# 32x32 block transposes on VectorE with a reorder through DRAM, in place of TensorE transposes, in an attention and feed-forward kernel; and one pinned order behind step 30

## The chip, the cores and the metric

The kernel runs on one core of a Trainium2 chip. TensorE (PE in the profile; PEld is its weight loads) writes its products to PSUM; VectorE (DVE), ScalarE (ACT) and GpSimd (POOL) work on tiles, each in the order of its own instruction stream; SyncE (SP) issues the transfers between DRAM and SBUF, also in order. The metric is the device time of one execution in microseconds, 657.18 us before the change.

## The reference

Attention in chunks, then a feed-forward layer with a rational activation, all in float32:

```python
for c in range(nc):                       # chunks of 32 queries
    q_c = q[:, :, c_start:c_end]
    k_full = concat([mem_k, k[:, :, l_start:r_end]])   # 8 + up to 16 + 32 + 8 keys
    scores = scale * (q_c @ k_full.T)
    a = exp(scores - max(scores)); a = a / (sum(a) + 1e-09)
    out[:, :, c_start:c_end] = a @ v_full
x = out.transpose(0, 2, 1, 3).reshape(3072, 512)
h = x @ w_in                              # 512 x 2048
P = a[0] + a[1]*h + a[2]*h**2 + a[3]*h**3
Q = 1 + abs(b[0])*abs(h) + abs(b[1])*h**2
y = (P / (Q + 1e-6)) @ w_out              # 2048 x 512
```

There are 4 batches of 8 heads, 768 positions and head size 64.

## The kernel before

**Blocks, units, steps.** The 3072 rows are cut into eight blocks of 384. A block needs its attention output, transposed, as four tiles of 128 channels by 384 rows; each comes from one unit, which is a pair of heads (i, p): block i, pair p. A step n is one pair of a block and a slice j of 128 of the 2048 hidden features; `order` lists the 128 steps: ten slices of block 0, ten of block 1, all 16 of block 2, the rest of blocks 1 and 0, and then blocks 3 to 7, 16 steps each (block 3 begins at step 48, block 7 at step 112).

**One step.** `g1(n)` is a set of 12 matmuls (`h`, L368): four channel tiles by three products, since x and w are each split into a high and a low part of type float32r, and low by low is left out. A chain then makes the activation out of h, 128x384, in these parts: `chain_abs` (ACT: ha = |h|, L419, and cy from it, L420), `chain_below` (POOL: cy times ha, L424), `chain_line` (ACT: ct, L429), `chain_above` (DVE, L433, L434), `chain_inverse` (ACT: Ln, L438, then Exp, L439), `chain_ratio` (DVE: L443 to L445), `chain_hi` (POOL: ghi, L450) and `chain_lo` (POOL: glo = ct - ghi, L457). `g2(n)` is a set of nine matmuls (`o`, L383), three for each 128 rows: ghi by w_hi, ghi by w_lo, glo by w_hi. They add up over a block's slices in three banks of PSUM; at a block's end `evac` takes them to the output.

**One unit.** `b` (`att_scores`, L264): 12 matmuls, one for each chunk of 32 queries, each on a strip of 32 columns of TensorE (`tile_position=(0, j * CHUNK)`), into one bank as 128x384; chunk c goes to strip c mod 4 (`g, j = divmod(c, 4)`). `m` (`att_max`): DVE masks, takes the maximum, subtracts. `x` (`att_exp`): ACT. `c` and `k` (`att_turn`, L291, and `att_keep`, L296): three 128x128 transposes on TensorE into PSUM and a copy by ACT give eT. `d` (`att_values`, L306): 12 matmuls on strips, as in b. `n` (`att_norm`): three DVE instructions give xt. `e` (`att_back`, L324): three TensorE transposes into PSUM. `h` (`att_hi`, L328): ACT rounds to x_hi. `l` (`att_lo`, L339): DVE takes x_lo = x - x_hi. Units of block 3 and later read q and k from one SBUF slot, and v from two buffers, loaded by SP.

**What sets the order.** Up to step 29 a list written out by hand (`SEQ`) gives the order of every instruction, and `pin` holds it. It covers the attention of blocks 0 to 2. From `HAND = 30` on each step emits `g1(n + 1)`, the chain's parts for n, n - 1 and n - 2, the units' stages that `plan` has put there (from `BASES`, `EARLY`, `OFFS` and, for block 5 on, `first[i] - LEAD + 4 * p`, four steps apart) and `g2(n - 2)`; there the instructions have priorities only, and the scheduler of the tile framework decides the order on each engine and in SP's queue.

Of the kernel before, what the change touches and what calls it, by code (L numbers as in the profile page):

```python
# [12 lines left out]
F32 = mybir.dt.float32  # L13
# [3 lines left out]
ALU = mybir.AluOpType  # L17
# [34 lines left out]
GHI_POOL = 200  # L52
LOAD_AT = [-2, -1]
EARLY = {1: [0, 1, 2, 3], 2: [0, 2, 2, 2], 3: [0, 1, 1, 3], 4: [0, 2, 3, 6]}
# [5 lines left out]
OFFS = [0, 3, 4, 4]  # L60
BASES = {1: [-2, 0, 1, 2], 2: [4, 6, 8, 10], 3: [34, 36, 40, 42], 4: [38, 45, 49, 54]}
# [3 lines left out]
def attn_moe(ctx, tc, qk, vm, w, a, b, out):  # L65
# [125 lines left out]
    def x_move(store):  # L191
        for d, t in zip(x_keep, (xh[0], xl[0])):
            if store:
                load(d.bitcast(F32), t.bitcast(F32))
            else:
                nc.gpsimd.dma_start(out=t, in_=d)
# [50 lines left out]
    turn = [0]  # L247

    def pa(i):
        turn[0] = (turn[0] + 1) % 4  # L250
        if i == 0:
            if turn[0] == 3:
                return ps_r.tile([P, 512], F32, name="pa", tag="cr")
            return ps_o.tile([P, DM], F32, name="pa", tag=f"o{turn[0]}")
        return ps_a.tile([P, 512], F32, name="pa", tag="pa0" if pinned[0] else "pa")

    def att_scores(i, p):
        u = unit[i, p]
        users[qk_slot(i, p)] = users.get(qk_slot(i, p), 0) - 1
        s = u["s"] = pa(i)  # L260
        sv = s[:, :NG * 2 * KEYS].rearrange("x (g h w) -> x g h w", g=NG, h=2)
        for c in range(NC):
            g, j = divmod(c, 4)
            pin(nc.tensor.matmul(sv[j * CHUNK:(j + 1) * CHUNK, g], lhsT=u["q"][c],  # L264
                                 rhs=u["k"][c], start=True, stop=True, tile_position=(0, j * CHUNK)))
# [19 lines left out]

    def att_turn(i, p):
        u = unit[i, p]
        ep = u["ep"] = pa(i)
        e = u.pop("e")
        for g in range(NG):  # L290
            pin(nc.tensor.transpose(out=ep[:, g * P:(g + 1) * P], in_=e[:, g], identity=ident))  # L291

    def att_keep(i, p):
        u = unit[i, p]
        eT = u["eT"] = at.tile([P, TB], F32, name="eT", tag="eT")
        pin(nc.scalar.copy(eT, u.pop("ep")[:, :TB]))  # L296

    def att_values(i, p):
        u = unit[i, p]
        if i == 0 and p >= 2:  # L300
            users[V_SLOTS[p - 2]] -= 1
        o = u["o"] = pa(i)
        ov = o[:, :NG * 2 * (D + 1)].rearrange("x (g h d) -> x g h d", g=NG, h=2)
        for c in range(NC):
            g, j = divmod(c, 4)
            pin(nc.tensor.matmul(ov[j * CHUNK:(j + 1) * CHUNK, g],  # L306
                                 lhsT=u["eT"][:, c * CHUNK:(c + 1) * CHUNK], rhs=u["v"][c],
                                 start=True, stop=True, tile_position=(0, j * CHUNK)))
# [10 lines left out]
    def att_back(i, p):  # L319
        u = unit[i, p]  # L320
        xp = u["xp"] = pa(i)
        xt = u.pop("xt")
        for g in range(NG):
            pin(nc.tensor.transpose(out=xp[:, g * P:(g + 1) * P], in_=xt[:, 2 * g:2 * g + 2, :], identity=ident))  # L324

    def att_hi(i, p):
        u = unit[i, p]
        pin(nc.scalar.copy(xh[i][:, p, :], u["xp"][:, :TB]))  # L328
        if i < XL_POOL:
            xf = u["xf"] = at.tile([P, TB], F32, name="xf", tag="xf")  # L330
            pin(nc.scalar.copy(xf, u.pop("xp")[:, :TB]))

    def att_lo(i, p):
        u = unit.pop((i, p))
        hi = xh[i][:, p, :].bitcast(F32)
        if i < XL_POOL:
            pin(nc.gpsimd.tensor_tensor(xl[i][:, p, :], u["xf"], hi, op=ALU.subtract))
        else:
            pin(nc.vector.tensor_tensor(xl[i][:, p, :], u["xp"][:, :TB], hi, op=ALU.subtract))  # L339

    def together(*parts):
        def f(i, p):
            for part in parts:
                part(i, p)
        return f

    att_d, att_e = together(att_values, att_norm), together(att_back, att_hi, att_lo)
    stages = [together(att_scores, att_max, att_exp), together(att_turn, att_keep), att_d, att_e]
# [22 lines left out]
    def g2(n):  # L371
# [7 lines left out]
        for t in range(NG):  # L379
            cols = slice(t * P, (t + 1) * P)  # L380
            o = outs[i][t]
            for m, (gt, wt) in enumerate(((hi, w_hi), (hi, w_lo), (lo, w_hi))):
                ins = nc.tensor.matmul(o, lhsT=gt[:, cols], rhs=wt, start=begin and m == 0, stop=end and m == 2)  # L383
                if pinned[0] or n == total - 1:
                    tc.keep_in_program_order(ins)
        if end and not pinned[0]:
            evac(i, j)

    def evac(i, j):
        for t in range(NG):  # L390
            if j < NJT - 1:
                if t == 0:
                    spare = slot(SPARES[i], "spare", F32, NG * DM)
                y = spare[:, t * DM:(t + 1) * DM]
            else:
                y = st.tile([P, DM], F32, name="stage", tag="stage")
            r = i * TB + t * P
            rows = slice(t * P, (t + 1) * P)
            if j < NJT - 1:
                pin(nc.scalar.mul(y, outs[i][t], 1.0 / W_SCALE))  # L400
                nc.sync.dma_start(out=part[i][rows, :], in_=y)
                continue
            if i < 2:
                nc.sync.dma_start(out=y, in_=part[i][rows, :])
                nc.vector.scalar_tensor_tensor(y, outs[i][t], 1.0 / W_SCALE, y, op0=ALU.mult, op1=ALU.add)
            elif i < NBLK - 1:
                nc.scalar.mul(y, outs[i][t], 1.0 / W_SCALE)
            else:
                half = DM // 2
                nc.scalar.mul(y[:, :half], outs[i][t][:, :half], 1.0 / W_SCALE)  # L410
                nc.vector.tensor_scalar(y[:, half:], outs[i][t][:, half:], 1.0 / W_SCALE, None, op0=ALU.mult)
            nc.sync.dma_start(out=out[r:r + P, :], in_=y)
        del outs[i]
# [40 lines left out]
    def chain_lo(z):  # L454
        glo = gl[z] = gp.tile([P, TB], F32R, name="glo", tag="glo")
        engine = nc.gpsimd if z < total - 1 else nc.vector
        pin(engine.tensor_tensor(glo, chain.pop(z)["t"], gh[z].bitcast(F32), op=ALU.subtract))  # L457

    def step(n):
        for lag, parts in ((2, (chain_hi, chain_lo)), (0, (chain_abs, chain_below, chain_line, chain_above)), (1, (chain_inverse, chain_ratio))):  # L460
            if 0 <= n - lag < total:
                for part in parts:
                    part(n - lag)
# [11 lines left out]
    x_free = {i: last[i - 2] - 1 if i > 1 else -2 for i in range(NBLK)}  # L475

    att, used = {}, {}

    def plan(at_step, rank, f, i, p):
        att.setdefault(at_step, []).append((rank, f, i, p))  # L480

    for i in range(3, NBLK):
        for p, base in enumerate(BASES.get(i, [first[i] - LEAD + 4 * p for p in range(NPAIR)])):
            offs = EARLY.get(i, OFFS)
            buf = qk_slot(i, p)
            at_qk = max(HAND, base + LOAD_AT[0], used.get(buf, -2))
            at_v = max(HAND, base + LOAD_AT[1], used.get(("v", p % 2), -2))
            plan(at_qk, 10, att_load, i, p)
            plan(max(at_qk, at_v), 11, att_loadv, i, p)
            floor = at_qk + 1  # L490
            for d, f in enumerate(stages):
                if f is att_d:
                    floor = max(floor, at_v + 1)
                if f is att_e:
                    floor = max(floor, x_free[i])
                floor = max(floor, base + offs[d])
                plan(floor, len(stages) - d, f, i, p)
                if d == 0:
                    used[buf] = floor
                if f is att_d:  # L500
                    used["v", p % 2] = floor
                floor += 1

    def attention_slot(n):
        for _, f, i, p in sorted(att.get(n, []), key=lambda e: (e[0], e[3])):
            f(i, p)
# [25 lines left out]
    paired = dict(b=att_scores, m=att_max, x=att_exp, c=att_turn, k=att_keep, d=att_values, n=att_norm, e=att_back, h=att_hi, l=att_lo)  # L532
    convert = dict(w=lambda key: w_load(*key), A=w_abs, B=w_bits, H=w_hi, L=w_lo)

    def hand(token):
# [3 lines left out]
        if where and kind in paired:  # L539
            paired[kind](i, p)  # L540
# [26 lines left out]
    def emit(step, offset, f, *args):  # L567
        tc.cur_priority = 8000 + 300 * step + offset
        f(*args)

    for n in range(HAND, total + LAG):
        tc.cur_priority = 8000 + 300 * n
        if n + 1 < total:
            g1(n + 1)
        step(n)
        emit(n, PA, attention_slot, n)
        tc.cur_priority = 8000 + 300 * n + 180
        if n - LAG >= 0:
            g2(n - LAG)
# [43 lines left out]
```

## Time and profile before

| | us |
|---|---|
| median of 3 executions | 657.18 (656.86 to 659.78) |
| the profiled execution, its time | 656.87 |
| its span, first to last instruction | 655.1 |
| TensorE busy (matmuls) | 628.3 (96%) |
| VectorE busy | 467.5 (71%) |
| ScalarE busy | 426.5 (65%) |
| GpSimd busy | 413.9 (63%) |
| mean granted TensorE clock | 0.987 |

The profile is of one execution. In a row of a timeline stand the start and the duration in us, the engine, the line of the kernel, the operation, out<-in, shapes, a count where instructions are merged, and in brackets the idle time ahead with what ended it. A matmul's duration is longer than its distance to the next one, since matmuls overlap: what a set costs TensorE is read from the starts. In a row of windows stand, after the length, each engine's busy time with its number of instructions, the granted clock, the share of the DMA engines that is busy and GB/s. In a row of a group stand the total busy time, the mean of one in ns, and idle time ahead. A float32 matmul of the program (not float32r) stands in the trace as two MATMUL records.

### The profile page before, as it was taken

How to read it: one execution, taken by the hardware profiler on the slowest of the kernel's cores; microseconds unless marked ns; L12 is line 12 of the kernel's file. 1: busy time of each engine (PE TensorE's matmuls, PEld its weight loads, DVE VectorE, ACT ScalarE, POOL GpSimd, SP SyncE). 2: the span in 40 equal slices, each digit the busy share in tenths (PEclk: the TensorE clock that was granted, in tenths of full speed). 3: DMA queues.
4: the chain of work that ended last, by engine and by line, in shares of the span. 5: the costliest groups of instructions: out<-in, count | busy, mean ns of one | idle time of the engine just before them, and what ended most of it. 6: DMA issues, size and time to landing. Idle time of an engine off the chain costs nothing.

```text
span 655.1 us, 12177 instructions
## 1 busy us (share of the span) xinstructions
PE 628.3 (96%) x4432; PEld 548.9 (84%) x4432; DVE 467.5 (71%) x940; ACT 426.5 (65%) x833; POOL 413.9 (63%) x439
## 2 busy tenths in 40 slices
PE   4689999999999999999999999999999999999997
PEld 3477787889988888878888888888888988999995
DVE  4878998997957577587677667666756766666664
ACT  3677878778855666466656756566656666666663
POOL 5557776878957666436665565656656565666663
PEclk8879999999999999999999999999999999999999
DMA  7998137304021524251211112213101300001001
GB/s 252 371 404 270 61 93 239 111 25 177 4 71 32 197 87 140 80 170 61 62 62 62 53 57 62 61 62 109 51 23 50 110 1 0 2 1 49 1 2 49
DMA packets 20525, 61.81 MB, mean 94 GB/s; under 512 B 3441, under 2 KB 3441, under 8 KB 20081
## 3 DMA queue, kind: packets, MB, share of 16 engines
q1 hardware_dynamic: 19856, 58.66, 26.4%
q0 software_dynamic: 288, 1.57, 0.7%
q8 instruction: 35, 0.57, 0.4%
q10 hardware_dynamic: 320, 0.80, 0.3%
q14 instruction: 26, 0.20, 0.1%
HBM read 51.58 MB, written 9.44 MB: 93 GB/s over the span
## 4 chain that ended last, share of the span: by engine, by line
PE 86%; DVE 7%; DMA 3%; issue 2%; ACT 1%; SPq 0%; DVEq 0%; ACTq 0%
PE h L368 40%; PE o L383 39%; PE pa L264 3%; PE pa L306 3%; DMA qk<-in_qk_dram 2%; PE pa L291 1%; DVE stage L169 1%; PE pa L324 1%; DVE w_raw L170 1%; DMA w_raw<-in_w_dram 1%; DVE mx L277 1%; DVE ct L433 1%; DVE ct L443 0%; DVE cr L444 0%; DVE ct L445 0%
## 5 line engine op out<-in xcount | busy, mean ns | idle before, releaser
L368 PE MATMUL h<-x_hi,w_hl 128*128 128x384 f32 x1024 | 268.5, 342 | 3.4 <-DVE ct L434 3.1
L383 PE MATMUL o<-w_hl,ghi 128*128 128x512 f32 x768 | 240.7, 398 | 0.0
L424 POOL TENSOR_TENSOR cy<-cy,ha 128x384 f32<-128x384 f32 x128 | 130.0, 1016 | 133.4 <-ACT cy L420 131.0
L368 PEld LDWEIGHTS h<-x_hi,w_hl 128*128 128x128 f32 x1024 | 187.7, 190 | 15.0 <-DVE ct L434 4.5
L368 PE MATMUL h<-x_lo,w_hl 128*128 128x384 f32 x512 | 174.1, 340 | 0.0
L383 PEld LDWEIGHTS o<-w_hl,ghi 128*128 128x128 f32 x768 | 140.2, 188 | 27.2 <-issue 4.0
L383 PE MATMUL o<-w_hl,glo 128*128 128x512 f32 x384 | 148.5, 398 | 0.0
L450 POOL TENSOR_TENSOR ghi<-ct,zero 128x384 fp32r<-128x384 f32 x127 | 105.0, 827 | 62.0 <-DVE ct L445 29.5
L457 POOL TENSOR_TENSOR glo<-ct,ghi 128x384 fp32r<-128x384 f32 x127 | 129.0, 1016 | 8.0 <-PE o L383 0.3
L443 DVE SCALAR_TENSOR_TENSOR ct<-ct,par,cr 128x384 f32<-128x384 f32 x128 | 78.2, 611 | 78.0 <-ACT cr L439 77.3
L438 ACT ACTIVATE cr<-cy 128x384 f32<-128x384 f32 x128 | 63.3, 495 | 96.2 <-POOL cy L424 65.3
L433 DVE TENSOR_TENSOR ct<-ct,h 128x384 f32<-128x384 f32 x128 | 70.2, 549 | 54.6 <-ACT ct L429 51.2
L419 ACT ACTIVATE ha<-h 128x384 f32<-128x384 f32 x128 | 62.9, 491 | 58.4 <-PE h L368 51.3
L368 PEld LDWEIGHTS h<-x_lo,w_hl 128*128 128x128 f32 x512 | 97.0, 189 | 0.4 <-issue 0.2
L420 ACT ACTIVATE cy<-ha,bab 128x384 f32<-128x384 f32 x128 | 90.6, 708 | 1.1
L429 ACT ACTIVATE ct<-h,par 128x384 f32<-128x384 f32 x128 | 85.2, 667 | 0.6 <-POOL glo L457 0.6
L383 PEld LDWEIGHTS o<-w_hl,glo 128*128 128x128 f32 x384 | 71.7, 188 | 16.4 <-issue 1.0
L434 DVE SCALAR_TENSOR_TENSOR ct<-ct,par,h 128x384 f32<-128x384 f32 x128 | 78.2, 612 | 3.0
L445 DVE SCALAR_TENSOR_TENSOR ct<-cr,ct 128x384 f32<-128x384 f32 x128 | 71.1, 555 | 3.0
L444 DVE SCALAR_TENSOR_TENSOR cr<-cy,cr 128x384 f32<-128x384 f32 x128 | 71.1, 555 | 0.4
L439 ACT ACTIVATE cr<-cr 128x384 f32<-128x384 f32 x128 | 61.2, 478 | 3.4
L183 POOL TENSOR_TENSOR w_hl<-w_raw,w_hl 128x512 fp32r<-128x512 f32 x32 | 41.9, 1311 | 23.8 <-ACT w_hl L178 22.8
(54 smaller groups left out, 422.1 us busy)
## 6 DMA issues: line engine op xcount, KB each, us to landing
qk<-in_qk_dram SPq DMA_DIRECT2D x64, 288.0 KB, 3.9
w_raw<-in_w_dram SPq DMA_DIRECT2D x26, 512.0 KB, 7.3
v_main<-in_vm_dram SPq DMA_DIRECT2D x56, 195.0 KB, 3.0
out_dram<-stage SPq DMA_DIRECT2D x24, 256.0 KB, 2.2
w_raw<-in_w_dram SPq DMA_DIRECT2D x3, 1024.0 KB, 4.8
part<-spare SPq DMA_DIRECT2D x6, 256.0 KB, 2.2
stage<-part SPq DMA_DIRECT2D x6, 256.0 KB, 2.8
v_first<-in_vm_dram SPq DMA_DIRECT2D x4, 195.0 KB, 4.4
```

The costliest lines, as they stand in the source:

```text
L368: pin(nc.tensor.matmul(h[:, :TB], lhsT=wt[:, cols], rhs=xt[i][:, ct, :], start=m == 0, stop=m == last))
L383: ins = nc.tensor.matmul(o, lhsT=gt[:, cols], rhs=wt, start=begin and m == 0, stop=end and m == 2)
L420: pin(nc.scalar.activation(c["y"], c["ha"], AF.Identity, scale=B1, bias=B0))
L424: pin(nc.gpsimd.tensor_tensor(c["y"], c["y"], c.pop("ha"), op=ALU.mult))
L429: pin(nc.scalar.activation(c["t"], c["h"], AF.Identity, scale=A3, bias=A2))
L433: pin(nc.vector.tensor_tensor(t, t, h, op=ALU.mult))
L434: pin(nc.vector.scalar_tensor_tensor(t, t, A1, h, op0=ALU.add, op1=ALU.mult))
L443: pin(nc.vector.scalar_tensor_tensor(t, t, A0, r, op0=ALU.add, op1=ALU.mult))
L444: pin(nc.vector.scalar_tensor_tensor(r, yy, QC, r, op0=ALU.add, op1=ALU.mult))
L445: pin(nc.vector.scalar_tensor_tensor(t, r, 2.0, t, op0=ALU.subtract, op1=ALU.mult, reverse0=True))
L450: pin(nc.gpsimd.tensor_tensor(ghi, chain[z]["t"], zero.broadcast_to([P, TB]), op=ALU.add))
L457: pin(engine.tensor_tensor(glo, chain.pop(z)["t"], gh[z].bitcast(F32), op=ALU.subtract))
```

## The change

For blocks 3 to 7 (`BLOCKWISE = 3`) the six TensorE transposes of a unit go. `c` and `e` each become one VectorE instruction that transposes every 32x32 block of a 128x384 tile in place of its position (`turn_blocks`), a store of the result to DRAM and four loads of 32 partitions (`across`), which put the blocks where a full transpose would have put them. So that this works out, chunk c goes to strip c // 3 in these blocks (`place`). `k` is gone; `h` reads the loaded tile; `l` moves from VectorE to GpSimd.

```diff
+BLOCKWISE = 3
+BASES = {3: [31, 33, 36, 38], 4: [42, 46, 50, 54]}
+WHEN = dict(b=0, m=0, x=1, c=1, d=5, n=5, e=6, h=9, l=9)
+SOON = {3: dict(d=4, n=4, e=5, h=8, l=8), 4: dict(h=8, l=8)}
+XB = {"xf": 2}
...
+    def place(i, c):
+        return divmod(c, 4) if i < BLOCKWISE else (c % NG, c // NG)
+
+    def across(blocks, name):
+        kept = dr.tile([P, TB], F32, name=name, tag=name, bufs=2)
+        load(kept, blocks)
+        t = at.tile([P, TB], F32, name=name, tag=name, bufs=XB.get(name, 1))
+        n = TB // 4
+        for b in range(4):
+            load(t[b * CHUNK:(b + 1) * CHUNK].rearrange("k (j n) -> k j n", n=n),
+                 kept.rearrange("(j k) (b n) -> b k j n", k=CHUNK, n=n)[b])
+        return t
...
-            g, j = divmod(c, 4)
+            g, j = place(i, c)
...
+    def turn_blocks(src):
+        t = at.tile([P, TB], F32, name="blocks", tag="blocks", bufs=2)
+        pin(nc.vector.transpose(out=t.rearrange("x (b g k) -> x b g k", b=4, g=NG), in_=src.rearrange("x g (b k) -> x b g k", b=4)))
+        return t
...
     def att_turn(i, p):
         u = unit[i, p]
+        if i >= BLOCKWISE:
+            u["eT"] = across(turn_blocks(u.pop("e").rearrange("x g w h -> x g (w h)")), "eT")
+            return
...
     def att_back(i, p):
         u = unit[i, p]
+        if i >= BLOCKWISE:
+            u["xp"] = across(turn_blocks(u.pop("xt").rearrange("x (g h) d -> x g (h d)", h=2)), "xf")
+            return
...
+        elif i >= BLOCKWISE:
+            pin(nc.gpsimd.tensor_tensor(xl[i][:, p, :], u["xp"][:, :TB], hi, op=ALU.subtract))
...
-        if z < min(GHI_POOL, total - 1):
+        if z < total - 2:
...
-        engine = nc.gpsimd if z < total - 1 else nc.vector
+        engine = nc.gpsimd if z < total - 2 else nc.vector
```

Behind step 30 everything is pinned now, the transfers too, in the order of the loop below. `attend(n, ...)` emits the stages that `WHEN` and `SOON` put at step n, counted from the unit's base; at the end of a block the loop also places `evac`, and `fetch` for the partial sums of blocks 0 and 1.

```diff
-    pinned[0] = in_order[0] = False
...
     for n in range(HAND, total + LAG):
...
+        g2(n - 2)
+        attend(n, "db")
+        attend(n, "qv")
+        if n + 1 < total - 1:
+            g1(n + 1)
...
+            chain_abs(n)
+            chain_below(n)
+            chain_line(n)
...
+            chain_above(n)
...
+            chain_inverse(n)
...
+            chain_ratio(n)
+        if n < total - 1:
+            chain_hi(n - 1)
+            chain_lo(n - 1)
+        attend(n, "xhlencm")
```

TensorE's stream in the attention of a late block, before: the three transposes of one unit (`e` is its input) between an h set and an o set, and further on the values of that unit and the scores of the next in the middle of an o set.

```order
L368 MATMUL h<-x_lo_105,w_hl 128x384
L291 MATMUL pa<-ident,e 128x128 x3
L383 MATMUL o_5289<-w_hl,ghi 128x512 x2
...
L383 MATMUL o_5290<-w_hl,ghi 128x512
L306 MATMUL pa<-v_main_101,eT 32x130 x12
L264 MATMUL pa<-qk 32x128 x12
L383 MATMUL o_5290<-w_hl,ghi 128x512
```

TensorE's stream at such a place now: the scores of one unit (L276) between an o set and an h set, and one step later the values (L328) of the unit ahead of it.

```order
L401 MATMUL o_5351<-w_hl,glo 128x512
L276 MATMUL pa<-qk 32x128 x12
L386 MATMUL h<-x_hi_103,w_hl 128x384 x2
...
L401 MATMUL o_5351<-w_hl,glo 128x512
L328 MATMUL pa<-v_main_101,eT 32x130 x12
L386 MATMUL h<-x_hi_103,w_hl 128x384 x2
```

The transposes are gone, and scores and values no longer stand next to each other; over the whole stream behind step 31, 17 such neighbours were there before and one is there now.

GpSimd's stream in the same stage, before: one of the three instructions of each step after the other, with no x_lo.

```order
L424 TENSOR_TENSOR cy<-cy,ha 128x384
L450 TENSOR_TENSOR ghi<-ct,zero 128x384
L457 TENSOR_TENSOR glo<-ct,ghi 128x384
L450 TENSOR_TENSOR ghi<-ct,zero 128x384
L424 TENSOR_TENSOR cy<-cy,ha 128x384
```

GpSimd's stream now, with x_lo of a unit (`xf` is the tile loaded from DRAM) behind the glo of every fourth step.

```order
L447 TENSOR_TENSOR cy<-cy,ha 128x384
L473 TENSOR_TENSOR ghi<-ct,zero 128x384
L480 TENSOR_TENSOR glo<-ct,ghi 128x384
L364 TENSOR_TENSOR x_lo_104<-xf,x_hi_102 128x384
L447 TENSOR_TENSOR cy<-cy,ha 128x384
L473 TENSOR_TENSOR ghi<-ct,zero 128x384
```

The order of the three is fixed: cy of step n, then ghi and glo of step n - 1; and x_lo is new there.

SyncE's queue in that stage, before: only the loads of v and of q and k, two halves each.

```order
L116 DMA v_main_100<-in_vm_dram 64x780 x2
L116 DMA qk<-in_qk_dram 64x1152 x2
L116 DMA v_main_101<-in_vm_dram 64x780 x2
L116 DMA qk<-in_qk_dram 64x1152 x2
L116 DMA v_main_100<-in_vm_dram 64x780 x2
```

SyncE's queue now; `blocks` is VectorE's output, the second eT and xf the tile in DRAM.

```order
L115 DMA qk<-in_qk_dram 64x1152 x2
L115 DMA v_main_100<-in_vm_dram 64x780 x2
L115 DMA eT<-blocks 128x384
L115 DMA eT<-eT 32x4x96 x4
L115 DMA xf<-blocks 128x384
L115 DMA xf<-xf 32x4x96 x4
```

Ten transfers a unit have come into the queue behind the loads that were there.

More of the change, by code (lines that the diff above doesn't have):

```diff
@@ L195, in x_move @@
             else:
-                nc.gpsimd.dma_start(out=t, in_=d)
+                pin(nc.gpsimd.dma_start(out=t, in_=d))
     unit = {}
@@ L383, in g2, with fetch @@
                 ins = nc.tensor.matmul(o, lhsT=gt[:, cols], rhs=wt, start=begin and m == 0, stop=end and m == 2)
[L384 to L389, printed above, removed]
-        for t in range(NG):
+                pin(ins)
+    kept = []
+    def fetch(i):
+        for t in range(NG):
+            y = st.tile([P, DM], F32, name="stage", tag="stage")
+            load(y, part[i][t * P:(t + 1) * P, :])
+            kept.append(y)
@@ L391, in evac @@
+    def evac(i, j, tiles=range(NG)):
+        for t in tiles:
+            rows = slice(t * P, (t + 1) * P)
+            o = outs[i][t]
             if j < NJT - 1:
                 if t == 0:
-                    spare = slot(SPARES[i], "spare", F32, NG * DM)
-                y = spare[:, t * DM:(t + 1) * DM]
+                    spares[:] = [slot(SPARES[i], "spare", F32, NG * DM)]
+                y = spares[0][:, t * DM:(t + 1) * DM]
+                pin(nc.scalar.mul(y, o, 1.0 / W_SCALE))
+                load(part[i][rows, :], y)
+                continue
+            if i < 2:
+                y = kept.pop(0)
+                pin(nc.vector.scalar_tensor_tensor(y, o, 1.0 / W_SCALE, y, op0=ALU.mult, op1=ALU.add))
@@ L395, in evac @@
             else:
                 y = st.tile([P, DM], F32, name="stage", tag="stage")
[L397 to L411, printed above, removed]
@@ L412, in evac @@
-            nc.sync.dma_start(out=out[r:r + P, :], in_=y)
-        del outs[i]
+                if i < NBLK - 1:
+                    pin(nc.scalar.mul(y, o, 1.0 / W_SCALE))
+                else:
+                    half = DM // 2
+                    pin(nc.scalar.mul(y[:, :half], o[:, :half], 1.0 / W_SCALE))
+                    pin(nc.vector.tensor_scalar(y[:, half:], o[:, half:], 1.0 / W_SCALE, None, op0=ALU.mult))
+            load(out[i * TB + t * P:i * TB + (t + 1) * P, :], y)
+    spares = []
@@ L504, in attention_slot, with plan @@
-    def attention_slot(n):
-        for _, f, i, p in sorted(att.get(n, []), key=lambda e: (e[0], e[3])):
-            f(i, p)
+    x_free = {i: max(last[m] for m in range(i) if m % 2 == i % 2) for i in range(2, NBLK)}
+    att = {}
+    pieces = dict(b=att_scores, m=att_max, x=att_exp, c=att_turn, k=att_keep, d=att_values, n=att_norm, e=att_back, h=att_hi, l=att_lo)
+    def plan(n, kind, i, p):
+        att.setdefault((n, kind), []).append((i, p))
+    units = [(i, p, base) for i in range(3, NBLK)
+             for p, base in enumerate(BASES.get(i, [first[i] - LEAD + 4 * p for p in range(NPAIR)]))]
@@ new lines, in attn_moe @@
+    went = []
+    for m, (i, p, base) in enumerate(units):
+        at_n = {kind: base + off for kind, off in {**WHEN, **SOON.get(i, {})}.items()}
+        if m >= 2:
+            at_n["e"] = max(at_n["e"], went[m - 2]["h"])
+        at_n["h"] = at_n["l"] = max(at_n["h"], at_n["e"] + 2, x_free[i])
+        went.append(at_n)
+        for kind, n in at_n.items():
+            plan(n, kind, i, p)
+        plan(max(HAND, went[m - 1]["b"]) if m else HAND, "q", i, p)
+        plan(max(HAND, went[m - 2]["d"]) if m >= 2 else HAND, "v", i, p)
@@ L508, in begin, with attend @@
+    def attend(n, kinds):
+        for kind in kinds:
+            for i, p in att.get((n, kind), ()):
+                if kind == "q":
+                    att_load(i, p)
+                elif kind == "v":
+                    att_loadv(i, p)
+                else:
+                    pieces[kind](i, p)
     def begin():
@@ L538, in hand @@
             i, p = int(where[0]), int(where[1])
-        if where and kind in paired:
-            paired[kind](i, p)
+        if where and kind in pieces:
+            pieces[kind](i, p)
         elif kind in single:
```

89 lines of the change are left out of this document (31 added, 58 removed).

## The prediction

> **What bounds the kernel now.** First the page: who is busy, and what the chain that ended last is made of.
>
> ```profile
> PE 628.3 (96%) x4432; PEld 548.9 (84%) x4432; DVE 467.5 (71%) x940; ACT 426.5 (65%) x833; POOL 413.9 (63%) x439
> PE 86%; DVE 7%; DMA 3%; issue 2%; ACT 1%; SPq 0%; DVEq 0%; ACTq 0%
> ```
>
> TensorE carries 86% of the chain. Then the windows, for a stretch of the late blocks.
>
> ```profile
> 436.00:457.80 21.80, 21.80 (x153) 19.27 (x152) 14.97 (x32) 14.79 (x30) 12.21 (x14) 1.00 0.32 108
> ```
>
> TensorE has no gap in it at full clock; VectorE has 6.8 us of 21.8 free, ScalarE 7.0, GpSimd 9.6. So behind step 30 time is saved only by what TensorE no longer issues or waits for, and lost only if something makes it wait. Then the timeline of one step without attention.
>
> ```profile
> 575.28 0.63 PE L383 MATMUL o<-w_hl,ghi 128*128 128x512 f32 x2
> 575.48 0.49 ACT L419 ACTIVATE ha<-h 128x384 f32<-128x384 f32 x1 [0.41 <-PE h L368]
> 575.74 0.40 PE L383 MATMUL o<-w_hl,glo 128*128 128x512 f32 x1
> ...
> 576.42 0.70 ACT L420 ACTIVATE cy<-ha,bab 128x384 f32<-128x384 f32 x1
> 577.20 1.02 POOL L424 TENSOR_TENSOR cy<-cy,ha 128x384 f32<-128x384 f32 x1 [1.29 <-ACT cy L420]
> 577.36 0.51 PE L368 MATMUL h<-x_hi,w_hl 128*128 128x384 f32 x2
> 578.18 0.82 POOL L450 TENSOR_TENSOR ghi<-ct,zero 128x384 fp32r<-128x384 f32 x1
> 578.25 0.50 ACT L438 ACTIVATE cr<-cy 128x384 f32<-128x384 f32 x1 [1.13 <-POOL cy L424]
> 578.78 0.47 ACT L439 ACTIVATE cr<-cr 128x384 f32<-128x384 f32 x1
> 579.08 1.01 POOL L457 TENSOR_TENSOR glo<-ct,ghi 128x384 fp32r<-128x384 f32 x1
> 579.29 0.61 DVE L443 SCALAR_TENSOR_TENSOR ct<-ct,par,cr 128x384 f32<-128x384 f32 x1 [1.40 <-ACT cr L439]
> 579.47 0.63 PE L383 MATMUL o<-w_hl,ghi 128*128 128x512 f32 x2
> 580.41 0.56 DVE L445 SCALAR_TENSOR_TENSOR ct<-cr,ct 128x384 f32<-128x384 f32 x1
> ```
>
> The o set (575.28 to 577.36) and the h set make a step of 4.19 us. Two ghi matmuls take 0.46 (575.28 to 575.74), so 0.23 for one. The glo that ends at 580.09 is too late for the third matmul at 579.93 and serves the set after it: GpSimd is some 4 us ahead.
>
> **Transposes that go.** The timeline around one TensorE transpose, a set of three.
>
> ```profile
> 463.69 0.34 PE L368 MATMUL h<-x_lo,w_hl 128*128 128x384 f32 x1
> 463.86 0.49 PE L291 MATMUL pa<-ident,e 128*128 128x128 f32 x3
> 464.11 0.71 PE L383 MATMUL o<-w_hl,ghi 128*128 128x512 f32 x2
> 464.65 0.39 PE L383 MATMUL o<-w_hl,glo 128*128 128x512 f32 x1
> ```
>
> The three take 0.25 us (463.86 to 464.11), and the next two o matmuls 0.54 in place of 0.46: 0.33 a set. There are 20 units with two sets, 40 x 0.33 = 13.2; I take 0.2 off for sets that stood next to each other and paid the 0.08 once. **-13.0 us**, all on TensorE's stream and so on the path.
>
> **Scores and values that are parted.** In the program they stood next to each other 17 times behind step 31, now once. First the timeline of a pair, then that of values alone.
>
> ```profile
> 450.24 0.63 PE L383 MATMUL o<-w_hl,glo 128*128 128x512 f32 x2
> 450.80 0.87 PE L306 MATMUL pa<-v_main,eT 128*32 128x130 f32 x24
> 451.49 0.84 PE L264 MATMUL pa<-qk 128*32 128x128 f32 x24
> 452.26 0.73 PE L383 MATMUL o<-w_hl,ghi 128*128 128x512 f32 x2
> 452.82 0.39 PE L383 MATMUL o<-w_hl,glo 128*128 128x512 f32 x1
> ...
> 545.34 0.39 PE L383 MATMUL o<-w_hl,ghi 128*128 128x512 f32 x1
> 545.65 0.87 PE L306 MATMUL pa<-v_main,eT 128*32 128x130 f32 x24
> 546.46 0.50 PE L383 MATMUL o<-w_hl,ghi 128*128 128x512 f32 x1
> 546.79 0.39 PE L383 MATMUL o<-w_hl,glo 128*128 128x512 f32 x1
> ```
>
> The pair: 450.24 to 452.82 is 2.58 with four o matmuls in it, 2.58 - 0.92 = 1.66. Alone: 545.34 to 546.79 is 1.45 with two, 1.45 - 0.46 = 0.99. Parting a pair costs 2 x 0.99 - 1.66 = 0.32, and 16 fewer pairs cost 16 x 0.32: **+5.1 us**. It could only be nothing if two sets alone were as cheap as a pair, which these rows exclude.
>
> **The new order of strips.** Three chunks in a row now go to the same strip. Windows over the start of the set at 450.80, with its instructions alone, show how strips run.
>
> ```profile
> 450.79:450.83 0.04, 0.03 (x4) 0.03 (x5) 1.00 0.00 0
> 450.83:450.93 0.10, 0.10 (x4) 0.10 (x8) 1.00 0.00 0
> 450.93:450.97 0.04, 0.04 (x8) 0.04 (x8) 1.00 0.00 0
> ```
>
> The second column after the length counts the matmuls in flight: four start within 0.04 us, none in the next 0.10, then four more. A set is six such rounds of 0.11. In the built program the two passes of one product stand next to each other and use the same strip, so strict order would have let no second strip start before the second pass of the first. I read it as strips that take work from the stream independently, and a strip has the same six passes as before: cost 0. The upper bound is the first rival.
>
> The Trainium skill (TensorE: Matmul & The Clock Gate, Part 3, The mechanism) speaks against the change here: matmuls are a strict first-in first-out in start and end, and only weight loads are pulled ahead. By that rule the sum would be that of the first rival; the rounds of four above speak against it.
>
> **Waits that go.** The timeline of block 3's one long gap.
>
> ```profile
> 282.60 0.49 PE L324 MATMUL pa<-ident,xt 128*128 128x128 f32 x3
> 284.52 0.55 PE L291 MATMUL pa<-ident,e 128*128 128x128 f32 x3 [1.44 <-ACT e L284]
> 285.21 0.62 PE L368 MATMUL h<-x_hi,w_hl 128*128 128x384 f32 x2
> ```
>
> Two sets next to each other would take 0.5, here 2.6: 2.1 us waiting for the exponential ahead of a transpose. No such transpose is left, and the values come three steps or more behind the exponential. **-2.1 us.**
>
> **The tighter chain.** What is late next? Now the chain's h comes at the start S of an o set, and glo of the step before is read in the *next* o set: GpSimd's lead of 4 us is given up. From the step above, with cy right behind ha: ha S+0.20, cy S+0.72 to 1.42, cy times ha on GpSimd S+1.50 to 2.52, ghi 2.48 to 3.30, glo 3.38 to 4.39. The third matmul of the next set stands at S + 4.19 + 0.46 = 4.65. So a step without attention leaves 0.26 us, less one hop of about 0.05 (GpSimd's end at 578.22, ScalarE's start at 578.25): **0.2 us to spare**. Scores or values add 0.99 in their step. ghi needs VectorE's ratio of the step before; Ln starts at S+2.55, Exp 0.53 later (578.25 to 578.78) and ends at S+3.55, and VectorE's three take 1.68 (579.29 to 580.97), so the ratio ends at S+5.3, 1.4 us ahead of S + 4.19 + 2.48. At a block's end three evacuations on ScalarE stand in the way; only behind block 6 does no set lengthen the step, and I add **+0.3 us** once.
>
> **VectorE, GpSimd and the transfers.** Nearest rows:
>
> ```profile
> L339 DVE TENSOR_TENSOR x_lo<-pa,x_hi 128x384 fp32r<-128x384 f32 x28 | 15.5, 554 | 16.2 <-ACT x_hi L328 15.2 <-PE h L368 1.0
> out_dram<-stage SPq DMA_DIRECT2D x24, 256.0 KB, 2.2
> stage<-part SPq DMA_DIRECT2D x6, 256.0 KB, 2.8
> w_raw<-in_w_dram SPq DMA_DIRECT2D x26, 512.0 KB, 7.3
> 226.34 1.33 SPq L412 DMA_DIRECT2D out_dram<-stage  x3
> ```
>
> A block transpose of 128x384 I take at 0.55 us, like L339; between nothing and twice that, the ratio's 1.4 us of lead covers it. GpSimd's new x_lo takes 1.0 (as glo) behind glo, S+4.4 to 5.4, in a step with values, whose next cy times ha comes at S+6.7: hidden. ScalarE loses a copy of eT. All cost 0. For the round trip: store 2.2, three issues of 0.44 ahead of the last load, its landing 2.8, together 6.3 us; with 7.3 for the load 10.8. From the transpose to the values there are four steps less what VectorE is behind, S+5.3 and up to four instructions like L339, 7.5: 4 x 4.19 + 2 x 0.99 + 2.1 - 7.5 = 13.3 us, in block 3 three steps and 9.1 us. The new waits: the values wait for the four loads of eT, and every matmul stands behind them; ScalarE's x_hi waits for xf, and the next ha stands behind it, 3 steps less 2 us after the transpose, over 10 us; in SP's queue the loads wait for the store, and those of q, k and v stand behind them, with a step or more to spare. I take 0; the upper end, 10.8 against 9.1 for each of block 3's four units, is +7.
>
> **The sum.** 655.1 - 13.0 + 5.1 - 2.1 + 0.3 = 645.4 us of span. Outside the span lie 1.8 us (656.87 against 655.1): 647.2. The profiled execution is 0.3 under the median of the runs shown, less than they scatter, so I leave **647.2 us**, 1.5% under 657.18.
>
> **Rivals.** *Strips in strict order (slower).* If TensorE starts matmuls in program order, six passes on one strip run one after the other and only the last overlaps the next strip: 24 - 3 = 21 rounds in place of 6, 15 x 0.11 = 1.65 a set, 40 sets, +66: 713 us; if half of that, 680. For it: the three chunks in a row. Against it: the four starts in 0.04 us. It decides as soon as a lone set costs over 1.2 us (0.2 x 40 = 8). Chance 0.11.
>
> *GpSimd's glo becomes the bound (no change).* The 0.2 us rests on four hops. If the chain is 0.4 longer than I work out, each step without attention grows by 0.2; there are about 60 from step 30 on (21 of them behind the last set), +12: 659.2. For it: GpSimd is busy 2.85 of 4.19 us in one piece and starts only on ScalarE's word. Against it: the durations repeat to 0.01 us from step to step. At 0.1 over what is to spare, +6, it gives 653.2. Chance 0.13.
>
> *The round trip is too long (slower).* If it needs 2 us more than 13.3, each of 20 units makes TensorE wait that long: +40, 687. For it: pieces of 384 B (96 words), of which no row here has a price. Against it: twice the worked-out 6.3 still fits. Chance 0.06.
>
> The Trainium skill (DMA: Bandwidth & Descriptors, Specifications) says that below 512 B a transfer is a read-modify-write and not at line rate; no row here prices it.
>
> **How the numbers follow.** The forecast has 0.66, the rivals 0.30, small things on both sides 0.04. About 0.5% is what a measurement of this kernel can tell from no change: under 653.9 is faster, over 660.5 slower. Faster: 0.66, a third of the glo case and 0.02 = 0.72. Slower: 0.11 + 0.06 + 0.01 = 0.18. Same: 0.10. The forecast's own range is 645.2 (a longer wait saved, no +0.3) to 654 (block 3's +7); to hold 8 in 10 the range goes up to 656.5, which takes in most of the glo case.
>
> **What would show it.** Right: no transposes among TensorE's rows; lone sets still at 0.99; TensorE at 21.8 of 21.8 in the late windows; a step of 4.19 in the last block; VectorE's STREAM_TRANSPOSE near 0.55; no wait of TensorE for eT. Wrong: a set of 24 records that lasts over 1 us; PE or PEld waiting for GpSimd's glo in block 7; waits for DMA ahead of the values, or ScalarE's x_hi waiting for xf.

## The result, and the profile after

The changed kernel takes **678.55 us**, the median of four executions (676.79 to 679.08), against 658.25 for the kernel before on the same chip (656.86 to 659.78): a ratio of 1.030, 95% interval 1.027 to 1.034. It is slower by 3%; 647.2 was predicted, 1.5% faster. The span of its profiled execution is 675.0 us, against 655.1.

From the page after, the busy time of the engines and the chain that ended last:

```profile
PE 646.6 (96%) x4312; PEld 562.6 (83%) x4312; DVE 496.6 (74%) x961; ACT 432.9 (64%) x814; POOL 430.8 (64%) x457
PE 41%; issue 24%; POOL 17%; DVE 6%; DMA 5%; ACT 4%; SPq 1%; POOLq 0%; ACTq 0%; DVEq 0%
```

TensorE runs 120 matmul records fewer than before (4312 against 4432: the transposes), and is busy 18 us longer. The chain looks as if GpSimd had become the bound (17%, before it was not in the row). It hadn't: the chain follows whatever released a step last, and glo now ends shortly ahead of its matmul (mostly by 0.23 to 0.26 us in a step without attention; 0.2 was worked out). What TensorE waited for behind step 30 stands in the list of its waits, in total us, times, longest:

```profile
PE pa L328 <- DMA eT<-eT: 1.9, 2, 1.3
PE o L401 <- ACT ghi L475: 0.3, 1, 0.3
PE o L401 <- DVE glo L480: 0.2, 1, 0.2
PE pa L328 <- PE o L401: 0.2, 1, 0.2
```

2.6 us in all, and none for GpSimd. The windows over the same stretch of time as before say the same: TensorE has no gap at full clock.

```profile
436.00:457.80 21.80, 21.80 (x149) 18.84 (x149) 15.02 (x30) 14.33 (x28) 13.57 (x15) 1.00 0.36 112
```

So the time is inside TensorE's own work. The timeline of TensorE around one lone set of scores (L276 is L264 of before):

```profile
450.94 0.39 PE L401 MATMUL o<-w_hl,glo 128*128 128x512 f32 x1
451.26 1.59 PE L276 MATMUL pa<-qk 128*32 128x128 f32 x24
452.77 0.62 PE L386 MATMUL h<-x_hi,w_hl 128*128 128x384 f32 x2
453.23 0.34 PE L386 MATMUL h<-x_lo,w_hl 128*128 128x384 f32 x1
...
453.75 0.33 PE L386 MATMUL h<-x_lo,w_hl 128*128 128x384 f32 x1
```

Three h matmuls take 0.52 (453.23 to 453.75), so 0.173 for one. From the o matmul at 450.94 to the h matmul at 453.23 it is 2.29; less one o (0.23) and two h (0.35) that is **1.71 for the set, where a lone set took 0.99 before**. Sets of values cost much the same (1.73 to 1.75, worked out likewise).

The windows of this set's first moments, with its instructions alone, against the three such rows that the prediction shows of before (the number in brackets behind the first column counts the matmuls in flight; one lasts 0.27 and its strip starts the next after 0.11, so up to three of a strip are counted):

```profile
451.25:451.29 0.04, 0.03 (x1) 0.04 (x2) 0.00 (x0) 0.00 (x0) 1.00 0.21 58
451.29:451.38 0.09, 0.09 (x1) 0.09 (x2) 0.00 (x0) 0.00 (x0) 1.00 0.05 9
451.38:451.42 0.04, 0.04 (x2) 0.04 (x2) 0.00 (x0) 0.00 (x0) 1.00 0.03 10
451.49:451.53 0.04, 0.04 (x4) 0.04 (x3) 0.00 (x0) 0.00 (x0) 1.00 0.00 0
451.74:451.78 0.04, 0.04 (x7) 0.04 (x5) 0.00 (x0) 0.00 (x0) 1.00 0.00 0
```

Before, four strips start within 0.04 us and then all four again. Now one strip starts, and for 0.24 us it stays alone; the first matmul of the second strip comes just behind the third of the first strip (0.248 behind the set's start), the third strip's at 0.497, the fourth's at 0.745. Three such delays are 0.74, and that is what a set has grown by (0.72 to 0.73).

The parts that the prediction priced without a row are in the page's groups and its list of transfers:

```profile
L300 DVE STREAM_TRANSPOSE blocks<-xt 128x384 f32<-128x384 f32 x20 | 11.3, 567 | 0.0
```

```profile
eT<-blocks SPq DMA_DIRECT2D x20, 192.0 KB, 1.9
eT<-eT SPq DMA_DIRECT2D x80, 48.0 KB, 1.9
```

A block transpose takes 0.567 us, that of e as that of xt (0.55 was taken); the store lands after 1.9, a load of 48 KB in pieces of 384 B after 1.9.

### The profile page after: what moved, and what is told of

Same layout as the page of the kernel before. It is cut to its first block, busy times and chain, and to the rows that moved or that the text cites. A ratio compares the mean times of both kernels' runs of the same rounds, so it can differ in the third digit from the quotient of the medians.

```text
span 675.0 us, 12305 instructions
## 1 busy us (share of the span) xinstructions
PE 646.6 (96%) x4312; PEld 562.6 (83%) x4312; DVE 496.6 (74%) x961; ACT 432.9 (64%) x814; POOL 430.8 (64%) x457
## 4 chain that ended last, share of the span: by engine, by line
PE 41%; issue 24%; POOL 17%; DVE 6%; DMA 5%; ACT 4%; SPq 1%; POOLq 0%; ACTq 0%; DVEq 0%
PE h L386 19%; PE o L401 16%; POOL glo L480 7%; POOL ghi L473 6%; PE pa L276 3%; DMA w_raw<-in_w_dram 3%; PE pa L328 2%; POOL cy L447 2%; POOL x_lo L364 2%; DVE stage L168 1%; SPq L115 1%; DVE w_raw L169 1%; ACT cr L461 1%; ACT e L296 1%; ACT x_hi L353 1%
## 5 line engine op out<-in xcount | busy, mean ns | idle before, releaser
L386 PEld LDWEIGHTS h<-x_hi,w_hl 128*128 128x128 f32 x1024 | 185.7, 190 | 19.1 <-issue 8.4
L401 PE MATMUL o<-w_hl,glo 128*128 128x512 f32 x384 | 151.7, 395 | 0.2 <-DVE glo L480 0.2
```

The costliest lines, as they stand in the source:

```text
L386: pin(nc.tensor.matmul(h[:, :TB], lhsT=wt[:, cols], rhs=xt[i][:, ct, :], start=m == 0, stop=m == last))
```

## The experiments

**Theory A:** TensorE gets past a strip that is busy only so far; with three chunks in a row on one strip it stops, and the other strips stay empty. **Rival B:** the round trip through DRAM or the tighter chain from h to glo costs the time, and the longer sets only hide it. Ratios are to the kernel before on the same chip.

### Strips in turn

In both `att_scores` and `att_values`; which chunk goes to which strip stays:

```diff
-        for c in range(NC):
+        for c in sorted(range(NC), key=lambda c: place(i, c)):
```

> The changed kernel with one thing altered: the 12 products of scores and of values are issued strip by strip in turn (0, 1, 2, 3, 0, 1, ...) in place of 0, 0, 0, 1, 1, 1, ...; chunks, strips, transposes and transfers stay as they are. Theory A (TensorE looks only a little way ahead, so three chunks in a row on one strip keep the other strips empty): a set of 24 records goes back from 1.72 us (with what the next matmul pays) to 0.99, 40 sets x 0.73 = 29 us, span 675.0 - 29 = 646, time about 648. Rival B (the round trip through DRAM or the tight chain from h to glo in the pinned order makes TensorE wait, and the longer sets only hide it): the order of the strips changes nothing, 677 to 679, or the 29 us come back as waits of TensorE for eT or glo. In between, the chain was hidden by the longer sets: 650 to 665 with such waits in the rows.

Measured: **651.41 us, ratio 0.990 (0.987 to 0.993)**; span 649.7. The order in which twelve independent products are written is worth 4% of the kernel (0.990 against 1.030). Timeline of a set:

```profile
435.21 0.39 PE L401 MATMUL o<-w_hl,glo 128*128 128x512 f32 x1
435.53 0.86 PE L276 MATMUL pa<-qk 128*32 128x128 f32 x24
436.32 0.62 PE L386 MATMUL h<-x_hi,w_hl 128*128 128x384 f32 x2
436.77 0.34 PE L386 MATMUL h<-x_lo,w_hl 128*128 128x384 f32 x1
```

435.21 to 436.77 is 1.56, less 0.58 for the same three matmuls: 0.98, as before the change. Theory A holds; B falls as the cause, though the longer sets did hide some waiting. 648 was expected: the wait for eT has grown to more than twice that of the changed kernel, 3.4 of it ahead of one unit's values in block 3, the rest in block 4, and behind the longer wait TensorE's clock is halved for a while (1.6 us more, worked out below).

```profile
PE pa L328 <- DMA eT<-eT: 4.3, 2, 3.4
```

### The kernel before, grouped by strip

```diff
-        for c in range(NC):
+        for c in sorted(range(NC), key=lambda c: c % 4) if i >= 3 else range(NC):
```

> The kernel before with one thing altered: in blocks 3 to 7 the 12 products of scores and of values are issued grouped by strip (0, 0, 0, 1, 1, 1, 2, 2, 2, 3, 3, 3) in place of in turn; TensorE's transposes stay, and there is no round trip and no pinned order. Theory A: each of the 40 sets grows by 0.73, or where scores and values stand next to each other (17 pairs) the end of one overlaps the start of the next and a pair grows by about 1.0: before + 21 to + 30, 678 to 688. Rival B (transfers or the pinned order cost the time): no change, 656 to 660.

Measured: **681.9 us, ratio 1.036 (1.033 to 1.039)**. The order alone, with TensorE's transposes in place, no round trip and no pinned order, makes the kernel before slower than the changed one. A pair of values and scores in its timeline:

```profile
428.36 0.39 PE L383 MATMUL o<-w_hl,ghi 128*128 128x512 f32 x1
428.68 1.28 PE L306 MATMUL pa<-v_main,eT 128*32 128x130 f32 x20
429.69 0.30 PE L264 MATMUL pa<-qk 128*32 128x128 f32 x1
...
430.05 1.24 PE L264 MATMUL pa<-qk 128*32 128x128 f32 x20
431.21 0.50 PE L383 MATMUL o<-w_hl,ghi 128*128 128x512 f32 x1
431.55 0.40 PE L383 MATMUL o<-w_hl,glo 128*128 128x512 f32 x1
```

428.36 to 431.55 less two o matmuls: 2.73 for the pair, 1.66 before. The first scores start (429.69) while values are still to come on the last strip: the strips do run apart from each other, once the stream reaches them.

### Two in a row, and one strip first

The kernel in turn with other keys, for blocks 3 and later. First, strips 0, 0, 1, 1, 2, 2, 3, 3, 0, 1, 2, 3:

```diff
+        for c in sorted(range(NC), key=lambda c: (place(i, c)[0] // 2, place(i, c)[1], place(i, c)[0])) if i >= BLOCKWISE else range(NC):
```

> The changed kernel with the products issued in the order of strips 0, 0, 1, 1, 2, 2, 3, 3, 0, 1, 2, 3: at most two products, four passes, of one strip stand in a row. It tells two forms of theory A apart. A1 (each strip holds about four passes, one running and three waiting; the stream stops when the strip it comes to is full): four in a row just fit, a set costs 0.09 more than in turn, total 4 us over the kernel in turn, about 652. A2 (one look-ahead over all strips of some three to four waiting passes): a new strip starts each time that two passes of the one ahead are done, a set costs 0.28 more, total 11 us over the kernel in turn, about 659. Rival B: 677 to 679 as after.

Measured: **652.64 us, ratio 0.992 (0.989 to 0.995)**. The windows at the start of a set, its instructions alone:

```profile
436.36:436.42 0.06, 0.05 (x4) 0.05 (x6) 0.00 (x0) 0.00 (x0) 1.00 0.00 0
```

Four strips start at once again, though four passes (two float32 products of two passes each) of the first strip stand ahead of the second in the stream. A look-ahead shared by all strips falls: to start the fourth strip the stream had to get past nine passes that were waiting, three on each strip, where in the changed kernel five on one strip stop it. The set costs 0.03 more than in turn, less than either form expected (from the o matmul at 436.04 to the third h matmul at 437.63 it is 1.59, less 0.58: 1.01).

Then strips 0, 0, 0, 1, 2, 3, 1, 2, 3, 1, 2, 3:

```diff
+        for c in sorted(range(NC), key=lambda c: (place(i, c)[1] > 0, place(i, c)) if i >= BLOCKWISE else c):
```

> The changed kernel with the products issued in the order of strips 0, 0, 0, 1, 2, 3, 1, 2, 3, 1, 2, 3: only the first strip has three products, six passes, in a row. It tests how TensorE looks ahead, behind the run with two products in a row. If a strip holds four passes, the stream stops once, until strip 0 has two of its six behind it, 0.25 us, and the rest runs beside: each of 40 sets costs 0.25 more than in turn, + 10 us, about 661. If what counts is only how many neighbours share a strip (8 of 11 cost 0.73 in the changed kernel, here 2): 0.18 a set, + 7, about 658; but by that the run of two in a row (4 neighbours) had to cost 0.36 a set, and it cost some 0.03. If the look-ahead is over all strips together and long enough for the run of two in a row, nothing: 651.

Measured: **659.8 us, ratio 1.002 (1.001 to 1.004)**, 8 us over the kernel in turn. Timeline of a set and, in a second view, two windows in it:

```profile
441.30 0.39 PE L401 MATMUL o<-w_hl,glo 128*128 128x512 f32 x1
441.62 1.10 PE L276 MATMUL pa<-qk 128*32 128x128 f32 x24
442.65 0.62 PE L386 MATMUL h<-x_hi,w_hl 128*128 128x384 f32 x2
443.11 0.33 PE L386 MATMUL h<-x_lo,w_hl 128*128 128x384 f32 x1
```

```profile
441.61:441.65 0.04, 0.03 (x1) 0.04 (x2) 0.00 (x0) 0.00 (x0) 1.00 0.30 77
441.85:441.89 0.04, 0.04 (x6) 0.04 (x5) 0.00 (x0) 0.00 (x0) 1.00 0.00 0
```

441.30 to 443.11 less 0.58 is 1.23, 0.25 over a set in turn, where 0.25 was expected of a strip that holds four passes and 0.18 of counted neighbours. The second window shows how: three passes of the first strip have been started, and then the three others start together, 0.25 us behind the first. The changed kernel and these three runs (in turn, two in a row, one strip first) fit one rule: **a strip holds one running and three waiting passes; a fifth stops the stream for all strips until the next pass of that strip starts.** What exactly is held, the matmuls or their weight loads, these runs do not separate. Three float32 products in a row are six passes, so each strip but the last delays the next by two passes and a bit, 0.25.

### The transposes put back

The kernel in turn, with three transposes of a constant ahead of the h set at each of the 40 places, into the bank that the h set overwrites (added work that nothing reads):

```diff
+        for _ in range(idle):
+            for t in range(NG):
+                pin(nc.tensor.transpose(out=h[:, t * P:(t + 1) * P], in_=ident, identity=ident))
...
-            g1(n + 1)
+            g1(n + 1, len(att.get((n, "c"), ())) + len(att.get((n, "e"), ())))
```

> The kernel with strips in turn, and in blocks 3 to 7 for each of the 40 places where the transposes of before have gone, three TensorE transposes of a constant put back into the bank of h ahead of the h set, which overwrites them: added work that nothing reads. It measures what the transposes cost by themselves: by the prediction's term 40 x 0.33 = 13 us over the kernel in turn, about 661. If less than 8 us, TensorE has idle time there that hides them, and the gain of taking them away was overestimated; if over 16, they cost more than the 0.33 read from the row.

Measured: **662.72 us, ratio 1.007 (1.005 to 1.010)**, 11.3 over the kernel in turn, 9.4 in span. In the timeline:

```profile
451.21 0.39 PE L404 MATMUL o<-w_hl,glo 128*128 128x512 f32 x1
451.44 0.49 PE L382 MATMUL h<-ident 128*128 128x128 f32 x3
451.69 0.59 PE L389 MATMUL h<-x_hi,w_hl 128*128 128x384 f32 x2
452.12 0.34 PE L389 MATMUL h<-x_lo,w_hl 128*128 128x384 f32 x1
```

451.21 to 452.12 is 0.91, less one o and two h: 0.33, the predicted price. In 20 of the 40 places they stand right behind values and cost 0.29, since the matmul behind such a set starts late in any case: 12.4 together. Against that the wait for eT is 2.7 here and not 4.3, and the clock stays at 1.00 behind it, where the kernel in turn loses 1.6 (below): 12.4 - 1.6 - 1.6 = 9.2, against 9.4 of span. The term holds.

### Values next to scores, and the reload

Six runs on what the kernel in turn still loses. First, values one step earlier, next to the scores of the next unit, from block 4 on:

```diff
-WHEN = dict(b=0, m=0, x=1, c=1, d=5, n=5, e=6, h=9, l=9)
+WHEN = dict(b=0, m=0, x=1, c=1, d=4, n=4, e=6, h=9, l=9)
```

> The kernel with strips in turn, and the values of a unit (with the normalisation behind them) one step earlier from block 4 on, so that in 14 more places they stand next to the scores of the next unit. It measures the term for parting scores and values by itself. If the term is right (0.32 a pair, now read as 0.99 + 0.98 - 1.65): 14 x 0.32 = 4.5 us less than in turn, about 647. If the values one step earlier come before their eT has landed, the gain is eaten by waits of TensorE for eT in blocks 4 to 7: 650 to 660. If the price of the part is something that neighbours do not save: 651, no change.

Measured: **654.09 us, ratio 0.992 (0.989 to 0.995)**, no gain over in turn (0.990). A pair costs what it should (1.65 to 1.67 in the timeline), and what it saves is eaten, mostly in block 4, as the second theory had it, by the wait for eT:

```profile
PE pa L328 <- DMA eT<-eT: 9.6, 2, 5.9
```

The clock is at half behind both of these waits, for 3.4 and for 3.9 us of TensorE's work.

Second, the reload of block 0's x_hi and x_lo one step later:

```diff
-        if n == 2 * SPLIT + NJT:
+        if n == 2 * SPLIT + NJT + 1:
             x_move(False)
```

> The kernel with strips in turn, and the reload of block 0's x_hi and x_lo from DRAM (1.5 MB, GpSimd's queue) one step later. Theory: the 3.4 us for which TensorE waits for eT in block 3 come from this reload, during which the store of xf does not land for some 8 us and holds up SP's queue, with eT's store 3 us late in it; one step later it runs while nothing in the queue waits for a landing. Then the wait for eT goes from 4.3 us to under 1, about 3.5 us less: 648. Rival: the queue itself is too full in block 3 (v, three output stores, q and k ahead of eT), the reload does not matter, and the wait stays at 3 to 4 us: 651.

Measured: **651.9 us, ratio 0.990 (0.988 to 0.993)**: no gain, and a wait for eT of 3.3 where under 1 was expected, so the theory as put falls. SP's queue in the kernel in turn, and here:

```profile
222.01 0.34 SPq L115 DMA_DIRECT2D xf<-blocks  x1
230.41 1.73 SPq L115 DMA_DIRECT2D xf<-xf  x4
...
235.06 0.40 SPq L115 DMA_DIRECT2D eT<-blocks  x1
238.23 1.75 SPq L115 DMA_DIRECT2D eT<-eT  x4
```

```profile
223.47 0.34 SPq L115 DMA_DIRECT2D xf<-blocks  x1
225.38 1.74 SPq L115 DMA_DIRECT2D xf<-xf  x4
...
230.60 1.23 SPq L115 DMA_DIRECT2D eT<-blocks  x1
238.91 1.75 SPq L115 DMA_DIRECT2D eT<-eT  x4
```

The loads of a round trip stand behind its store. In turn, the store of xf is 8.4 us ahead of its loads and eT's 3.2; one step later it is 1.9 and 8.3. The 1.5 MB keep the transfers busy for some 8 us (with the reload later, the DMA engines are 0.9 to 1.1 busy from 230 to 238), and the reload moved from one round trip to the other. Both edits together:

> Strips in turn, values next to scores, and the later reload. If the two terms are independent, the sum: 4.5 + 3.5 = 8 us less than in turn, about 643.5, and 2.2% under the kernel before. If values next to scores make a step long enough that something else is late (glo, eT), less than the sum: 645 to 648, with such a wait in the rows.

Measured: **654.16 us, ratio 0.994 (0.992 to 0.996)**; the wait for eT is 6.7, and the clock is at half twice, for 6.8 us each time. Of the 8 us that were expected nothing is left: 4.5 from the pairs, against 2.4 more of waiting and the halved clock. So both were put elsewhere. Values earlier in blocks 5 to 7 alone (block 4 keeps its 5):

```diff
-WHEN = dict(b=0, m=0, x=1, c=1, d=5, n=5, e=6, h=9, l=9)
-SOON = {3: dict(d=4, n=4, e=5, h=8, l=8), 4: dict(h=8, l=8)}
+WHEN = dict(b=0, m=0, x=1, c=1, d=4, n=4, e=6, h=9, l=9)
+SOON = {3: dict(d=4, n=4, e=5, h=8, l=8), 4: dict(d=5, n=5, h=8, l=8)}
```

> Strips in turn, and values one step earlier than there in blocks 5 to 7 alone, so that 11 more places have them next to scores. In the run that did so from block 4 on, the waits of TensorE for eT grew from 4.3 to 9.6 us, all of it in blocks 3 and 4, where SP's queue is full; from step 48 to the end it was 4.2 us shorter. If parting costs 0.32 a pair: 11 x 0.32 = 3.5 us less than in turn, about 648, with the eT waits of 4.3 as they were. If the price were not real: 651.4.

Measured: **648.32 us, ratio 0.985 (0.982 to 0.987)**, 0.0056 less than in turn, 3.7 us. The timeline of a pair:

```profile
436.61 0.39 PE L401 MATMUL o<-w_hl,glo 128*128 128x512 f32 x1
436.93 0.87 PE L328 MATMUL pa<-v_main,eT 128*32 128x130 f32 x24
437.62 0.84 PE L276 MATMUL pa<-qk 128*32 128x128 f32 x24
...
438.85 0.35 PE L386 MATMUL h<-x_lo,w_hl 128*128 128x384 f32 x1
```

436.61 to 438.85 is 2.24, less 0.58 for one o and two h: 1.66 for the pair, as before the change. That the time came out as expected is in part luck: the wait for eT is 6.5 and not 4.3, and the clock, which stays at 1.00 behind it, gives 1.6 of that back. The reload one step *earlier* (`n == 2 * SPLIT + NJT - 1`):

> Strips in turn, and the reload of x_hi and x_lo one step earlier in place of one later. One step later it met the store of eT (landed after 8.3 us) in place of that of xf, and the wait for eT only went from 4.3 to 3.3. Theory (what lies in the way is 1.5 MB on DMA engines that are full for some 8 us, wherever they meet a round trip): one step earlier the 8 us are over before eT's store is ready at 231, and no eT store is in flight at the time; the wait goes to about 1, 3 us less than in turn, 648.5. It may meet the load of q and k for the third unit instead: then scores wait some 2 us, and 650. Rival (the queue's own length): the wait for eT stays at 3 to 4, 651.

Measured: **648.09 us, ratio 0.984 (0.981 to 0.987)**, 4.1 us less than in turn. No scores wait for q and k, and the wait for eT is down by a third:

```profile
PE pa L328 <- DMA eT<-eT: 2.9, 2, 1.5
```

That is 1.4 us, not 4, and the wait was to go to about 1. The windows of the kernel in turn behind its wait of 3.4 us show where the rest came from (the figure behind the engines is the granted clock of TensorE):

```profile
242.35:242.98 0.63, 0.63 (x7) 0.63 (x4) 0.43 (x3) 0.00 (x0) 0.00 (x0) 1.00 1.08 379
242.98:243.83 0.85, 0.85 (x5) 0.85 (x5) 0.48 (x1) 0.00 (x0) 0.00 (x0) 0.57 0.86 322
243.83:244.79 0.96, 0.96 (x5) 0.96 (x5) 0.00 (x0) 0.00 (x0) 0.00 (x0) 0.50 0.14 50
...
246.80:248.19 1.39, 1.39 (x7) 1.12 (x6) 0.38 (x1) 0.98 (x2) 0.89 (x1) 1.00 0.58 176
```

From 242.98 to 246.80 nine h and three o matmuls take 3.82 us; at 0.173 and 0.23 they would take 2.25. The clock was halved for some three us, and that costs 1.6 more than the wait. With the reload earlier the clock stays at 1.00 behind both waits: 1.4 + 1.6 = 3.0 of the 4.1 are accounted for. Three was expected too, but from the wait alone. Last, both:

> Both: values next to scores in blocks 5 to 7, the reload one step earlier. They touch different stretches (blocks 5 to 7; block 3), so the sum of the two: 3.5 + 3 = 6.5 us less than in turn, about 645, 2% under the kernel before; 648 if the reload gains nothing.

Measured: **646.04 us, ratio 0.980 (0.978 to 0.982)**: 2.0% faster than the kernel before, and 4.9% faster than the changed one (0.980 / 1.030). The wait for eT is 2.0. The round trip was worth having: it spares the 12.4 us that the transposes cost where they were put back, and costs this wait.

## Why the prediction was wrong

**The step that failed** is the new order of strips: "I read it as strips that take work from the stream independently, and a strip has the same six passes as before: cost 0." The row it rests on, four starts within 0.04 us, is right, and strips are independent. But it was read in a program where four strips alternate, so it shows that the stream gets past *two* passes of a busy strip, not past six. It gets past four and no further. The term was 38 lone sets x (1.71 - 0.98) = 27.7 and 1.1 for the one pair (as 2.73 - 1.66 in the kernel before, grouped), 28.8 in place of 0.

**The first rival** was this mechanism in its strict form (1.65 a set, 713 us), with 680 "if half of that"; the truth, 0.73 of 1.65, lies there. Its chance of 0.11 was too low: the only evidence against it came from the other order, and the change altered just that. The rule that stood with it, of matmuls that are strictly first in, first out (the Trainium skill, TensorE: Matmul & The Clock Gate, Part 3, The mechanism), is not what these runs show: with the passes of a product next to each other it would have cost 1.65 a set here, and 0.73 was measured; in the changed kernel the second strip starts behind three of the first strip's six passes, and in strips in turn the fourth strip starts 0.02 us behind the first.

**The other terms held.** Transposes that go: 0.33 a set, 12.4 to 13.0 in all. Parting: 0.32 a pair (two lone sets of 0.99 against 1.66 for the pair with neighbours late). The wait that goes, 2.1: gone. The tighter chain: TensorE never waited for GpSimd's glo, and the 0.3 behind block 6 did not come (there glo still ends 0.15 ahead of its matmul); at the very end TensorE waits 0.5 for ghi of ScalarE and glo of VectorE, which the sum did not have. The block transpose, ScalarE and x_lo: hidden; a step of the last block is 4.18 long (o sets at 609.20 and, four steps on, 625.92). The round trip: taken as 0 with an upper end of +7 for block 3; it was 1.9 in the changed kernel and 5.9, with the clock, in turn. Of the three rivals the one on glo gave nothing. The one on the round trip had each of 20 units wait; two wait, in block 3 in the changed kernel and in blocks 3 and 4 in turn. Its reason was not the cause: pieces of 384 B land in 1.9 us, and for the longest wait it is the reload that is in the way. (The Trainium skill, DMA: Bandwidth & Descriptors, Specifications, has transfers below 512 B as read-modify-write and not at line rate; a load of 48 KB lands here after the same 1.9 as the store of the whole tile, 192 KB. What it would take in longer pieces no run here shows.)

**The sum, with the failed term replaced.** 645.4 is the predicted span; the last column is the start of the 29th o set, ahead of which these five kernels do not differ; what is left is the span less the sum:

| | sum | span | left | o set |
|---|---|---|---|---|
| after | 645.4 + 28.8 + 1.9 (eT) = 676.1 | 675.0 | -1.1 | 188.0 |
| in turn | 645.4 + 4.3 + 1.6 (clock) = 651.3 | 649.7 | -1.6 | 188.0 |
| earlier reload | 645.4 + 2.9 = 648.3 | 646.0 | -2.3 | 187.2 |
| neighbours late | 645.4 - 3.5 + 6.5 (eT) = 648.4 | 649.2 | +0.8 | 190.2 |
| both, last | 645.4 - 3.5 + 2.0 = 643.9 | 644.1 | +0.2 | 189.6 |

What is left goes with how late the execution is at step 28, before anything that differs: with each row's start taken off, the five agree within 0.5 us. The two late ones are late from the first o set of all (52.6 and 52.3, the others 50.3 to 51.0). Why was not tried. What also stays open is why the wait for eT differs between kernels whose queue has the same order up to block 5 (4.3 in turn, 6.5 with neighbours late).

## What to carry to other kernels

When a change alters the order in which independent pieces are issued, evidence that they overlap must come from an order like the new one: ask how many instructions the engine has to get past, not only whether it can. On column strips, write products so that the strip changes from one to the next; two float32 products in a row on a strip still let the next strip start at once, three don't. And a wait is to be priced with what it sets off behind it: a stop of 3.4 us of TensorE cost 5.0.

## What the runs showed of the hardware that was not expected

- **How deep a strip's queue is:** one pass running and three waiting; the fifth stops TensorE's stream for every strip (0.25 us a strip with six passes in a row, nothing with four).
- **The clock after a wait:** behind waits of 3.4 us (in turn), 2.6 us (reload later) and 2.5 us (one strip first) the granted clock fell to 0.5 for about three us; behind 3.1 us (neighbours late) and 2.0 us (transposes put back) it stayed at 1.00. The Trainium skill (TensorE: Matmul & The Clock Gate, Part 1) has the clock halved after an idle window of about 3.4 us, which runs by itself, and given back after a busy one. The traces agree with the window: in each of the 13 the clock changes only in steps of 3.41 us, and where these steps fall differs from run to run. They do not agree that the window has to be idle throughout. Behind step 30 the clock was halved after every window at full clock in which TensorE was idle, by the profile's modelled ends of matmuls, for 1.86 us or more (21 windows; from 239.69 to 243.10 in turn it is busy 1.55 of 3.41; from 238.40 to 241.81 with the reload later, 1.18) and after none with 1.81 us or less (from 241.70 to 245.11 with neighbours late it is busy 1.68). So 2.5 us are enough when most of them fall into one window, and 3.1 us are not when two windows share them.
- **One large transfer beside small ones:** while 1.5 MB were being loaded, a store of 192 KB that else lands in 1.9 us held up its loads for 8.3 us (reload later).
